# Decode attention and MLP on one core: the next head's softmax weights move behind the copy of the output column, and the scores use 4 stationary columns instead of 32

## The chip, the core and the metric

The kernel runs on one core of a Trainium2 chip. Its engines are TensorE (PE, with its weight loads shown apart as PEld), VectorE (DVE), ScalarE (ACT), GpSimd (POOL) and SyncE (SP), whose queue issues nearly all transfers here. The metric is device time in microseconds (us), lower is better. A profile is one execution with a hardware trace.

## The reference

Two layers of attention and MLP run one after the other, and then both again with the same weights: four token vectors (batch B = 4) of width D = 640, 32 heads of 128, the last W = 1024 cached keys and values of each head, everything in fp32.

```python
x = x + A(layernorm(x)); x = x + M(layernorm(x)); x = x + A(layernorm(x)); x = x + M(layernorm(x))
# A: q = (x @ wq) per head;  scores = q . k_cache[:, :, -1024:] * 128**-0.5
#    p = softmax(scores);    o = p @ v_cache[:, :, -1024:];   return o @ wo
# M: return relu(x @ w1) @ w2          (w1: 640 x 1728, w2: 1728 x 640)
```

## The kernel before

The host packs all that one head needs into a record: 9,472 fp32 columns on 128 partitions (4.85 MB), in the order WQ (640 columns), K (4,096), V (4,096), WO (640). Five records fit into SBUF (`slot0` to `slot4`), beside a `ring` of 8,960 columns that holds MLP weights and parts of one record.

The program makes two rounds (r = 0, 1) of attention and MLP. Round 0 takes heads 0 to 31. Round 1 begins with heads 27 to 31, which still lie in the slots, and then loads heads 0 to 26 again. All loads stand in one list, `items`, in a fixed order, and go to SP's queue: `pump()` issues the next one only when nothing live lies in its destination. `done(key, lo, hi)`, called behind the matmuls that used a piece, frees it and calls `pump()`. So a transfer can't begin before PE has used up what lies there, and all behind it in the list wait too. At the end of a round (`ending`) the last three records are split: K of head a, K of b, V of a, K of c, V of b, V of c in two halves; then come w1 in five pieces and w2. In round 0 the first five pieces of w1 and a bit of w2 fit into the ring; the rest of w2 needs the columns that the first MLP matmuls free.

Each engine executes in the order in which the code is written (`InOrder`). Per head, with n the position in the round:

- `query(n+2)`: 5 matmuls (10 as profiled: each fp32 matmul shows as two instructions) into `misc`, then DVE copies `misc` to `qT`.
- `scores(n+1)`: 8 matmuls into `sc_ps[(n+1) % 2]`, one column group of 32 partitions for each batch entry b. The stationary operand is column b of `qT` repeated 32 times, so that all 32 partitions of the group hold the same scores. DVE takes the maximum, ACT the exponential with its sum in `tot`.
- `weights(n+1)`: DVE takes the reciprocal of the sum, makes `mrt` from it, and transposes the exponentials in two halves (into PSUM `t_ps`, then scaled into `wT`).
- `values(n)`: 8 matmuls of `wT` with V into `o_ps`; then four DVE operations gather the column `on` out of `o_ps`.
- `output_T(i)`: a matmul of `on` with `pick`, and DVE's copy of the result to `oTs`; `project`: 4 matmuls of `oTs` with WO into `acc`, which frees the slot.

Around the MLP stand `center` (the mean for the layer norm) and `mlp`. `busy(n)` is a matmul with one stationary column and n moving columns whose result nobody uses. In round 0 the last 3 heads are projected behind the loop (`late`), in round 1 the last one.

Of the kernel before, what the change touches and what calls it, by code (L numbers as in the profile page):

```python
# [38 lines left out]
P = 128  # L39
# [53 lines left out]
def decode_kernel(ctx: ExitStack, tc: tile.TileContext, xf, rec, w1, w2, out):  # L93
    nc = tc.nc
    pe, dve, act, pool, sp = (InOrder(tc, e) for e in (nc.tensor, nc.vector, nc.scalar, nc.gpsimd, nc.sync))
# [5 lines left out]
    scratch = sb.tile([P, 480], F32, name="scratch")  # L101
    wT = scratch[:, :128].rearrange("p (i c j) -> p i c j", i=2, c=16)
    on = scratch[:, 128:256]
    xc = scratch[:, 256:256 + FD]
    x_sb = scratch[:, :FD]
    hT = scratch.rearrange("p (m j) -> p m j", j=32)
    oTs = sb.tile([P, LATE, B], F32, name="oTs")
    qT = sb.tile([P, B], F32, name="qT")
# [5 lines left out]
    nmax, rtot, rstd, eps, eps_dh, ones, unused, sums, squares, tot0, tot1 = (small[:, i:i + 1] for i in range(11))  # L114
    tot = [tot0, tot1]
# [3 lines left out]
    sc_ps = [ps.tile([P, W], F32, name=f"sc_ps{i}") for i in range(2)]  # L119
# [25 lines left out]
    dve.memset(eps_dh, EPS * DH)  # L145
    dve.memset(ones, 1.0)
    dve.memset(o_ps, 0.0)

    order = [list(range(H)), list(range(H - NS, H)) + list(range(H - NS))]
    LAST = H - NS  # L150

    def home(h, r):

        return h % NS if not r or h >= LAST else (h - 6 + LAST) % NS
# [30 lines left out]
    n = 0  # L185
# [24 lines left out]
    n = 0  # L210
# [18 lines left out]
    def cols(key, lo, n):  # L229

        for x, y, buf, col in pieces(key):
            if x <= lo and lo + n <= y:
                return buffers[buf][:, col + lo - x:col + lo - x + n]
        raise KeyError((key, lo, n))

    def done(key, lo, hi):

        if key[0] == "rec" and key[1] == 0 and key[2] >= LAST:
            return
        for x, y, buf, col in pieces(key):  # L240
            a, b = col + max(lo, x) - x, col + min(hi, y) - x
            if a < b:
                rest = []
                for bb, u, v in live:
                    if bb != buf or v <= a or b <= u:
                        rest.append((bb, u, v))
                    else:
                        rest += [(bb, p, q) for p, q in ((u, a), (b, v)) if p < q]
                live[:] = rest
        pump()  # L250


    def busy(n):

        pe.matmul(sc_ps[1][0:1, :n], mean_of[:, 0:1], slot[home(LAST, 0)][:, K:K + n], start=True, stop=True)

    def center(fill):

        x = acc[:, :FD]
        dve.tensor_reduce(sums, x, op=OP.add, axis=AX.X)  # L260
        if fill:
            busy(256)
        pe.matmul(misc[:, 0:1], mean_of, sums, start=True, stop=True)
        if fill:
            busy(512)
            busy(256)
        dve.tensor_scalar(xc, x, misc[:, 0:1], None, op0=OP.subtract)
        dve.transpose(xT, xc)
        act.activation(t_ps[:, :FD], xc, AF.Square, accum_out=squares)
# [7 lines left out]
    def scale_scores():  # L277

        pe.matmul(o_ps[:, 8:8 + B], ones.to_broadcast([P, P]), mrt, start=True, stop=True)
        dve.tensor_tensor(mrt, o_ps[:, 8:8 + B], of_batch, op=OP.mult)  # L280
        dve.tensor_reduce(sums, mrt, op=OP.add, axis=AX.X)
        act.activation(rstd, sums, AF.Sqrt, bias=eps_dh, scale=float(DH))
        act.activation(unused, eps, AF.Exp)
# [4 lines left out]
    def query(r, h):  # L288
        key = ("rec", r, h)
        for k in range(KB):  # L290
            pe.matmul(misc[:, 8:8 + B], cols(key, WQ + k * DH, DH), xblock(k), start=(k == 0), stop=(k == KB - 1))
        done(key, WQ, K)
        dve.tensor_copy(qT, misc[:, 8:8 + B])

    def scores(r, h, s, first=False):
        key = ("rec", r, h)
        for i in range(2):
            for b in range(B):
                pe.matmul(sc_ps[s][32 * b:32 * b + 32, 512 * i:512 * i + 512], qT[:, b:b + 1].to_broadcast([P, 32]),
                          cols(key, K + 512 * (B * i + b), 512), start=True, stop=True)  # L300
            done(key, K + VH * i, K + VH * i + VH)
        dve.tensor_reduce(nmax, sc_ps[s], op=OP.max, axis=AX.X, negate=True)
        if first:
            dve.reciprocal(rstd, rstd)
        dve.tensor_tensor(nmax, nmax, rstd, op=OP.mult)
        act.activation(sc_ps[s], sc_ps[s], AF.Exp, bias=nmax, scale=rstd, accum_out=tot[s])

    def weights(s):
        dve.reciprocal(rtot, tot[s])
        dve.tensor_scalar(mrt, of_batch, rtot, None, op0=OP.mult)  # L310
        for i in range(2):
            dve.transpose(t_ps, sc_ps[s][:, 512 * i:512 * i + 512])
            dve.tensor_tensor(wT[:, i], t_ps.rearrange("p (c j) -> p c j", j=32)[:, :, :B],
                              mrt.unsqueeze(1).to_broadcast([P, 16, B]), op=OP.mult)

    def values(r, h):
        key = ("rec", r, h)
        for i in range(2):
            for g in range(4):
                pe.matmul(o_ps[32 * g:32 * g + 16, :], wT[:, i, 4 * g:4 * g + 4, :].rearrange("p c j -> p (c j)"),  # L320
                          cols(key, V + VH * i + 512 * g, 512), start=(i == 0), stop=(i == 1))
            done(key, V + VH * i, V + VH * i + VH)
        dve.tensor_scalar(on, o_ps[:, :DH], of_block[:, 0:1], None, op0=OP.mult)
        for c in range(1, 4):
            dve.scalar_tensor_tensor(on, o_ps[:, DH * c:DH * c + DH], of_block[:, c:c + 1], on, op0=OP.mult, op1=OP.add)

    def output_T(i):
        pe.matmul(o_ps[:, :B], on, pick, start=True, stop=True)
        dve.tensor_copy(oTs[:, i], o_ps[:, :B])

    def project(r, h, i, end):
        key = ("rec", r, h)
        for n in range(NB):
            pe.matmul(acc[32 * n:32 * n + B, :FD], oTs[:, i], cols(key, WO + n * FD, FD),
                      start=False, stop=end, skip_group_check=True)
        done(key, WO, REC)
# [39 lines left out]
    for r in range(2):  # L376
        hs = order[r]
        late = LATE if r == 0 else 1
        center(r > 0)
        dve.tensor_scalar(mrt, mean_of[:, :B], squares, None, op0=OP.mult)  # L380
        query(r, hs[0])
        scale_scores()
        scores(r, hs[0], 0, True)
        query(r, hs[1])
        weights(0)
        for n, h in enumerate(hs):
            more = n + 1 < H
            i = n - (H - late)
            if more:
                scores(r, hs[n + 1], (n + 1) % 2)  # L390
            values(r, h)
            if more:
                weights((n + 1) % 2)
            if n + 2 < H:
                query(r, hs[n + 2])
            if i < 0:
                output_T(0)
                project(r, h, 0, False)
            elif more:
                output_T(i)  # L400
        for i in range(late):
            if i == max(0, late - 2):
                output_T(late - 1)
            project(r, hs[H - late + i], i, i == late - 1)
        center(True)
        mlp(r)
# [40 lines left out]
```

## Time and profile before

| | |
|---|---|
| median of 3 runs | 757.75 us (755.97 to 761.33) |
| the profiled execution | 753.13 us, span 751.4 us |
| PE busy | 538.2 us (72%) |
| DVE busy | 338.9 us (45%) |
| DMA, mean over the span | 304.48 MB, 405 GB/s |
| mean granted PE clock | 0.768 |

In the page's lines of slices each of 40 columns is 1/40 of the span (18.8 us); a digit is a share in tenths. In the table of windows the last three columns are the granted PE clock (1.00 is full speed), the busy share of the DMA engines and the bytes moved per time. In the timeline the columns are the start, the length, the engine, the instructions with their count, and in brackets the idle time of the engine just before with what ended it. Groups give the count, the busy time, the mean of one instruction in ns, and the idle time before them.

### The profile page before, as it was taken

The numbers are of one execution on the slowest core, as the hardware profiler recorded it, in microseconds if no ns is written. First come the engines' busy times: TensorE is split into PE (matmuls) and PEld (weight loads), VectorE is DVE, ScalarE is ACT, GpSimd is POOL, SyncE is SP. The second block draws the span as 40 slices with busy tenths as digits, with TensorE's granted clock in tenths as the row PEclk, the third lists the DMA queues.
The fourth block names the chain that finished last, engine by engine and source line by source line (L and its number), as shares of the span: only waits on it lengthen the run. The fifth ranks groups of instructions, "written<-read, shape, count | busy, mean of one in ns | idle before, by whom it ended". The sixth has DMA issues, their size and how long they took to land.

```text
span 751.4 us, 8825 instructions
## 1 busy us (share of the span) xinstructions
PE 538.2 (72%) x3704; PEld 222.6 (30%) x3704; DVE 338.9 (45%) x934; ACT 96.0 (13%) x154; POOL 1.1 (0%) x9
## 2 busy tenths in 40 slices
PE   3375686876676776777699777777776777776868
PEld 2132243233233232233224233323322233232312
DVE  2435535445535445345512655555555435345450
ACT  2101101101101101101111111111111101101111
POOL 0000000000000000000000000000000000000000
PEclk9768757677877678668679988868778757777689
DMA  9999999999999999999939997999999999999991
GB/s 388 426 441 420 442 428 420 446 423 428 437 424 437 431 422 443 424 424 423 387 125 407 366 432 319 414 428 422 440 427 432 432 424 437 431 426 424 423 420 64
DMA packets 15335, 304.48 MB, mean 405 GB/s; under 512 B 1712, under 2 KB 1984, under 8 KB 5312
## 3 DMA queue, kind: packets, MB, share of 16 engines
q1 hardware_dynamic: 15264, 303.91, 95.2%
q8 instruction: 29, 0.48, 0.3%
q14 instruction: 10, 0.08, 0.0%
q10 hardware_dynamic: 32, 0.01, 0.0%
HBM read 303.84 MB, written 0.08 MB: 404 GB/s over the span
## 4 chain that ended last, share of the span: by engine, by line
DMA 55%; PE 29%; DVE 13%; issue 1%; ACT 0%; another core or an unknown queue 0%
DMA slot<-rec 55%; PE sc_ps L85 13%; PE o_ps L85 8%; DVE scratch L85 6%; DVE t_ps L85 4%; PE acc L85 4%; PE misc L85 4%; DVE mrt L85 1%; DVE small L85 1%; DVE oTs L85 1%; ACT sc_ps L85 0%; DVE qT L85 0%; DVE sc_ps L85 0%
## 5 line engine op out<-in xcount | busy, mean ns | idle before, releaser
L85 PE MATMUL sc_ps<-slot,qT 128*32 128x512 f32 x992 | 200.6, 951 | 2.9 <-DVE oTs L85 2.0
L85 PE MATMUL misc<-xT,slot 128*128 128x4 f32 x620 | 98.7, 286 | 123.4 <-DMA slot<-rec 122.5
L85 DVE TENSOR_REDUCE small<-sc_ps 128x1 f32<-128x1024 f32 x64 | 78.4, 1224 | 233.6 <-PE sc_ps L85 233.6
L85 ACT ACTIVATE sc_ps<-sc_ps,small 128x1024 f32<-128x1024 f32 (+3 forms) x70 | 77.5, 1107 | 593.1 <-DVE small L85 571.0
L85 PE MATMUL o_ps<-slot,scratch 128*16 128x512 f32 x1010 | 149.8, 715 | 2.7 <-DVE oTs L85 1.9
L85 PEld LDWEIGHTS misc<-xT,slot 128*128 128x128 f32 x620 | 93.3, 233 | 178.5 <-DMA slot<-rec 160.0
L85 DVE STREAM_TRANSPOSE t_ps<-sc_ps 128x512 f32<-128x512 f32 x128 | 93.2, 728 | 2.2
L85 PE MATMUL acc<-slot,oTs 128*4 128x160 f32 x512 | 39.3, 393 | 54.5 <-DVE oTs L85 54.5
L85 PEld LDWEIGHTS o_ps<-slot,scratch 128*16 128x16 f32 x1010 | 37.4, 126 | 137.8 <-issue 131.8
L85 DVE SCALAR_TENSOR_TENSOR scratch<-o_ps,of_block,scratch 128x128 f32<-128x128 f32 x192 | 67.3, 351 | 6.8
L85 PEld LDWEIGHTS sc_ps<-slot,qT 128*32 128x32 f32 x992 | 43.6, 155 | 80.1 <-issue 71.9
L85 DVE TENSOR_SCALAR scratch<-o_ps,of_block 128x128 f32<-128x128 f32 x64 | 22.4, 350 | 50.6 <-PE o_ps L85 50.6
L85 PE MATMUL o_ps<-pick,scratch 128*128 128x4 f32 x128 | 29.1, 298 | 15.5 <-DVE scratch L85 15.5
L85 DVE COPY qT<-misc 128x4 f32<-128x4 f32 x64 | 10.1, 157 | 50.8 <-PE misc L85 50.5
L85 PEld LDWEIGHTS o_ps<-pick,scratch 128*128 128x128 f32 x128 | 25.5, 247 | 21.7 <-DVE scratch L85 21.7
L85 DVE TENSOR_TENSOR scratch<-t_ps,mrt 128x64 f32<-128x64 f32 x128 | 28.8, 225 | 4.4
L85 PE MATMUL sc_ps<-slot,mean_of 128*1 128x512 f32 (+1 forms) x54 | 26.2, 590 | 0.0
L85 PEld LDWEIGHTS acc<-slot,oTs 128*4 128x4 f32 x512 | 7.4, 85 | 61.5 <-DVE oTs L85 60.0
L85 DVE TENSOR_SCALAR mrt<-of_batch,small 128x4 f32<-128x4 f32 x64 | 14.7, 230 | 2.3
L85 DVE RECIPROCAL small<-small 128x1 f32<-128x1 f32 x68 | 10.4, 153 | 8.8 <-ACT small L85 7.5
L85 DVE COPY oTs<-o_ps 128x4 f32<-128x4 f32 x64 | 10.1, 158 | 7.7 <-PE o_ps L85 6.7
L85 ACT ACTIVATION_READ_ACCUMULATOR sc_ps<-sc_ps,small 128x1 f32 x64 | 12.2, 191 | 0.0
(53 smaller groups left out, 97.2 us busy)
## 6 DMA issues: line engine op xcount, KB each, us to landing
slot<-rec SPq DMA_DIRECT2D x46, 4736.0 KB, 30.7
slot<-rec SPq DMA_DIRECT2D x17, 2368.0 KB, 14.3
slot<-rec SPq DMA_DIRECT2D x5, 1024.0 KB, 33.1
ring<-w SPq DMA_DIRECT2D x5, 864.0 KB, 13.6
slot<-rec SPq DMA_DIRECT2D x2, 2048.0 KB, 40.3
slot<-rec SPq DMA_DIRECT2D x3, 1344.0 KB
slot<-w SPq DMA_DIRECT2D x3, 864.0 KB, 31.7
ring<-rec SPq DMA_DIRECT2D x1, 2368.0 KB
```

The costliest lines, as they stand in the source:

```text
L85: r = build(*args, **kwargs)
```

## The change

Three things change. In the loop over heads, `weights(n+1)` moves from before `query(n+2)` to the end of the iteration, behind `output_T` and `project`. The stationary operand of the scores has 4 columns instead of 32, so that only partitions 32b to 32b+3 get scores; the others are set to zero once at the start, and the sum of partition 32b is spread over its block by a 32x32 transpose of `tot` (read as 32 equal columns) into `spread`. And two `busy(512)` stand ahead of the last `output_T` of each round.

```diff
+    spread = scratch[:, 256:288]
...
+    for a in sc_ps:
+        dve.memset(a, 0.0)
...
-                pe.matmul(sc_ps[s][32 * b:32 * b + 32, 512 * i:512 * i + 512], qT[:, b:b + 1].to_broadcast([P, 32]),
+                pe.matmul(sc_ps[s][32 * b:32 * b + 4, 512 * i:512 * i + 512], qT[:, b:b + 1].to_broadcast([P, 4]),
...
     def weights(s):
-        dve.reciprocal(rtot, tot[s])
+
+        dve.transpose(spread, tot[s].to_broadcast([P, 32]))
+        dve.reciprocal(rtot, spread[:, 0:1])
         dve.tensor_scalar(mrt, of_batch, rtot, None, op0=OP.mult)
...
             values(r, h)
-            if more:
-                weights((n + 1) % 2)
             if n + 2 < H:
                 query(r, hs[n + 2])
             if i < 0:
                 output_T(0)
                 project(r, h, 0, False)
             elif more:
                 output_T(i)
+            if more:
+                weights((n + 1) % 2)
         for i in range(late):
             if i == max(0, late - 2):
+                busy(512)
+                busy(512)
                 output_T(late - 1)
             project(r, hs[H - late + i], i, i == late - 1)
```

On DVE, one head in the middle of round 0 stands like this before. The first rows are the four operations that gather the output column `on` (in `scratch`), the next six are `weights`, the last two the copies to `qT` and `oTs`.

```order
L85 TENSOR_SCALAR scratch<-o_ps,of_block 128x128
L85 SCALAR_TENSOR_TENSOR scratch<-o_ps,of_block,scratch 128x128 x3
L85 RECIPROCAL small<-small 128x1
L85 TENSOR_SCALAR mrt<-of_batch,small 128x4
L85 STREAM_TRANSPOSE t_ps<-sc_ps_78 128x512
L85 TENSOR_TENSOR scratch<-t_ps,mrt 128x64
L85 STREAM_TRANSPOSE t_ps<-sc_ps_78 128x512
L85 TENSOR_TENSOR scratch<-t_ps,mrt 128x64
L85 COPY qT<-misc 128x4
L85 COPY oTs<-o_ps 128x4
```

The same place on DVE after the change:

```order
L85 TENSOR_SCALAR scratch<-o_ps,of_block 128x128
L85 SCALAR_TENSOR_TENSOR scratch<-o_ps,of_block,scratch 128x128 x3
L85 COPY qT<-misc 128x4
L85 COPY oTs<-o_ps 128x4
L85 STREAM_TRANSPOSE scratch<-small 128x32
L85 RECIPROCAL small<-scratch 128x1
L85 TENSOR_SCALAR mrt<-of_batch,small 128x4
L85 STREAM_TRANSPOSE t_ps<-sc_ps_78 128x512
L85 TENSOR_TENSOR scratch<-t_ps,mrt 128x64
L85 STREAM_TRANSPOSE t_ps<-sc_ps_78 128x512
L85 TENSOR_TENSOR scratch<-t_ps,mrt 128x64
```

Both copies now stand directly behind the gathering, the weights stand behind the copies, and the small transpose of the sum is new.

On PE the order is unchanged but for the end of each round. At the end of round 0 it was, from the values of the last head on:

```order
L85 MATMUL o_ps<-slot_72,scratch 16x512 x8
L85 MATMUL acc<-slot_75,oTs 4x160 x4
L85 MATMUL o_ps<-pick,scratch 128x4
L85 MATMUL acc<-slot_71,oTs 4x160 x4
L85 MATMUL acc<-slot_72,oTs 4x160 x4
```

And after the change:

```order
L85 MATMUL o_ps<-slot_72,scratch 16x512 x8
L85 MATMUL acc<-slot_75,oTs 4x160 x4
L85 MATMUL sc_ps_78<-slot_73,mean_of 1x512 x2
L85 MATMUL o_ps<-pick,scratch 128x4
L85 MATMUL acc<-slot_71,oTs 4x160 x4
L85 MATMUL acc<-slot_72,oTs 4x160 x4
```

The two `busy` matmuls stand between the projection of the third last head and `output_T` of the last one. SP's and ACT's orders are the same in both.

## Prediction

> **What bounds the kernel now.** I read the page's slices, queues and chain first: which stage is bound by what.
>
> ```profile
> DMA  9999999999999999999939997999999999999991
> GB/s 388 426 441 420 442 428 420 446 423 428 437 424 437 431 422 443 424 424 423 387 125 407 366 432 319 414 428 422 440 427 432 432 424 437 431 426 424 423 420 64
> ...
> q1 hardware_dynamic: 15264, 303.91, 95.2%
> ...
> DMA 55%; PE 29%; DVE 13%; issue 1%; ACT 0%; another core or an unknown queue 0%
> ```
>
> Transfers run at 420 to 445 GB/s nearly everywhere: 303.91 MB at 426 are 713 us, 38 less than the span. So nothing can be won while the DMA is full, and all that can be won lies where it isn't: the dip in the middle (125, then 366 and 319), and the end (64). The windows price these places; the last column is GB/s, the third last the granted PE clock.
>
> ```profile
> 290.00:300.00 10.00, 7.30 (x56) 2.61 (x51) 5.14 (x14) 1.29 (x2) 0.00 (x0) 0.79 1.00 426
> 370.00:380.00 10.00, 5.34 (x36) 1.66 (x36) 4.99 (x15) 0.47 (x2) 0.00 (x0) 0.64 0.50 203
> 380.00:390.00 10.00, 10.00 (x61) 2.72 (x62) 1.38 (x5) 1.97 (x4) 0.00 (x0) 0.68 0.23 76
> 420.00:430.00 10.00, 7.57 (x64) 3.07 (x60) 5.03 (x14) 1.29 (x2) 0.00 (x0) 0.83 0.90 359
> 430.00:440.00 10.00, 7.57 (x64) 3.11 (x60) 5.04 (x14) 1.29 (x2) 0.00 (x0) 0.88 0.95 379
> 460.00:470.00 10.00, 7.51 (x68) 3.04 (x64) 5.88 (x15) 1.29 (x2) 0.00 (x0) 0.93 0.64 248
> 740.00:750.00 10.00, 7.82 (x125) 3.44 (x121) 1.16 (x4) 1.08 (x3) 0.00 (x0) 1.00 0.03 9
> ```
>
> A window at g GB/s loses 10 x (1 - g/426) us: 5.2 and 8.2 us between 370 and 390, 1.6, 1.1 and 4.2 us between 420 and 470. At the end PE works on without transfers. In all three places the DMA waits for PE to free space, or has nothing left. How long PE takes for a head there, the timeline shows (start, length, engine; in brackets the idle time before):
>
> ```profile
> 341.14 1.12 DVE L85 SCALAR_TENSOR_TENSOR scratch<-o_ps,of_block,scratch 128x128 f32<-128x128 f32 x3
> 342.18 0.15 DVE L85 RECIPROCAL small<-small 128x1 f32<-128x1 f32 x1
> 342.32 0.39 PE L85 MATMUL o_ps<-pick,scratch 128*128 128x4 f32 x2 [0.43 <-DVE scratch L85]
> 344.29 0.23 DVE L85 TENSOR_TENSOR scratch<-t_ps,mrt 128x64 f32<-128x64 f32 x1
> 344.50 0.15 DVE L85 COPY oTs<-o_ps 128x4 f32<-128x4 f32 x1
> 344.71 0.46 PE L85 MATMUL acc<-slot,oTs 128*4 128x160 f32 x8 [2.00 <-DVE oTs L85]
> 344.98 3.23 PE L85 MATMUL sc_ps<-slot,qT 128*32 128x512 f32 x16
> 363.94 2.79 PE L85 MATMUL sc_ps<-slot,qT 128*32 128x512 f32 x12 [2.02 <-DVE oTs L85]
> ```
>
> `output_T` on PE is over at 342.71, but DVE copies its result only at 344.50: `weights`, from the reciprocal at 342.18 on, stands ahead of the copy. PE stands for 2.00 us. From 344.71 to 363.94 two heads pass, 9.6 us each. Where DMA is the bound, the same wait is small, since `weights` is over before the next record lands:
>
> ```profile
> 275.60 1.28 PE L85 MATMUL misc<-xT,slot 128*128 128x4 f32 x10 [2.92 <-DMA slot<-rec]
> 277.35 0.71 PE L85 MATMUL acc<-slot,oTs 128*4 128x160 f32 x8 [0.26 <-DVE oTs L85]
> ```
>
> **The change, part by part.** *The move.* Behind it the projection should wait 0.26 us as in the last row, not 2.00: 1.74 us less per head that PE bounds. `weights` now runs while PE does the next `scores`. It takes 344.52 - 342.18 = 2.34 us, the first half of `wT` some 1.0 us earlier; the scores take 3.23 us here and 1.72 at full clock (below), with 0.46 of projection ahead. So `values` find their first half ready, just so at full clock. Where DMA bounds, PE waits 2.92 us per record and the weights fit under the scores: nothing. Queued behind the waiting copy on DVE is `weights` alone, and its reader, `values`, stands behind the scores on PE anyway.
>
> The second effect is the clock. Groups of three heads at the end of each round, and the same work at full clock out of the chain:
>
> ```profile
> L85 PE MATMUL sc_ps<-slot,qT 128*32 128x512 f32 x48 | 9.5, 930 | 2.0 <-DVE oTs L85 2.0
> L85 PE MATMUL o_ps<-slot,scratch 128*16 128x512 f32 x48 | 8.2, 811 | 0.0
> L85 PE MATMUL acc<-slot,oTs 128*4 128x160 f32 x16 | 0.9, 299 | 4.0 <-DVE oTs L85 4.0
> ...
> L85 PE MATMUL sc_ps<-slot,qT 128*32 128x512 f32 x48 | 9.2, 904 | 0.0
> L85 PE MATMUL o_ps<-slot,scratch 128*16 128x512 f32 x48 | 6.8, 696 | 0.0
> L85 PE MATMUL acc<-slot,oTs 128*4 128x160 f32 x24 | 1.9, 401 | 6.0 <-DVE oTs L85 6.0
> ```
>
> ```profile
> 716.49 1.72 PE sc_ps L85 x16
> 718.21 1.76 PE o_ps L85 x16
> ```
>
> At full clock three heads would take 3 x (1.72 + 1.76) = 10.4 us; they take 17.7 us at 344.7 to 370.3 and 16.0 at 695.1 to 720: 7.3 and 5.6 us go to the half clock. It follows the gap:
>
> ```profile
> 342.00:344.00 2.00, 0.39 (x2) 0.30 (x2) 1.90 (x6) 0.00 (x0) 0.00 (x0) 1.00 0.97 411
> 346.00:348.00 2.00, 2.00 (x16) 0.45 (x12) 0.00 (x0) 0.00 (x0) 0.00 (x0) 0.50 1.00 425
> 387.00:404.00 17.00, 16.33 (x169) 5.32 (x161) 1.32 (x5) 1.25 (x4) 0.00 (x0) 1.00 0.95 358
> ```
>
> PE idles at 342 to 344, and 2 us later the clock is 0.50. Without the gap I expect it to stay near 1.00. The Trainium skill, in "TensorE: Matmul & The Clock Gate", section "Why this matters for your kernels", has the clock fall only behind idle gaps of over about 3 us. By that rule gaps of 2.0 us would cost no clock and closing them would give none; the rows disagree. I keep it as a rival.
>
> *The first end (round 0).* Three waits (2.0 + 4.0 us in the group) give 3 x 1.74 = 5.2, the clock up to 7.3: 12.5. But the last V must land first.
>
> ```profile
> 332.10 2.30 PE misc L85 x10
> ...
> 374.17 3.61 PE L85 MATMUL o_ps<-slot,scratch 128*16 128x512 f32 x16 [1.94 <-DVE oTs L85]
> 379.41 0.59 PE L85 MATMUL o_ps<-pick,scratch 128*128 128x4 f32 x2 [1.10 <-DVE scratch L85]
> 386.64 0.33 SPq L85 DMA_DIRECT2D ring<-w  x1
> ...
> 682.34 1.42 PE L85 MATMUL misc<-xT,slot 128*128 128x4 f32 x10 [4.11 <-DMA slot<-rec]
> 724.15 3.51 PE L85 MATMUL o_ps<-slot,scratch 128*16 128x512 f32 x16
> ```
>
> At 332.10 the last whole record has landed. Behind it come three K parts (4,736 columns with WQ) and three V parts (4,096): 26,496 columns of 512 bytes, 13.57 MB, 31.9 us at 426 GB/s, so the last V lands at about 364 (an estimate). The last `values` start at 374.17, ten later than that. Their start behind `output_T`'s copy gains nothing (weights now follow the copy; the first half of `wT` is ready about when the copy was), so three waits it is, and I take 10.5 of the 12.5, between 5.2 (no clock) and 12. The first w2 transfer, issued at 386.64 when the MLP frees the ring, moves up as much. The queue, empty from about 376 on, then hardly runs dry.
>
> *Round 1.* In five heads from 416 to 457 the projection waits 10.1 us:
>
> ```profile
> L85 PE MATMUL acc<-slot,oTs 128*4 128x160 f32 x40 | 2.6, 335 | 10.1 <-DVE oTs L85 10.1
> ```
>
> 5 x 1.74 = 8.7 us, without any clock. The three dips there are 6.9 us in sum, and what ends each is a slot or the ring coming free behind these heads. I take 6.5, from 4 to 7. Then the DMA is full until the end.
>
> *The second end (round 1).* The same three waits, 5.2, and up to 5.6 of clock: 10.8. The landing bound: from 682.34, three K and three V parts, all with WO: 28,416 columns, 14.55 MB, 34.2 us, to 716.5; the last `values` start at 724.15, 7.6 later, and then run at half clock (3.51). I take 9, from 5 to 10, some of it being the end's clock. The DMA ends earlier than PE here, so the whole comes off the end.
>
> *The rest.* The new 128x32 transpose isn't in the trace; the nearest is
>
> ```profile
> L85 DVE STREAM_TRANSPOSE xT<-scratch 128x160 f32<-128x160 f32 x4 | 1.4, 345 | 0.1
> ```
>
> so at most 0.35 us, at least 0; I take 0.2, being a fifth of the columns with a fixed part. It lies under the scores; where it doesn't (the last weights of a round, two times) it costs 0.4 in all; uncovered in all of some 14 heads that PE bounds (4, 6 and 4 at the three places) it would cost up to 2.8 us more. The two memsets run while x is on its way at the start. The scores' 4 columns stream the same 512 moving columns: I take 0, a gain on the weight loads (off the path) or loss being possible only through the clock (rival three). The two `busy` fill the gap of 1.10 us ahead of 379.41: at half clock they take about 1.7 (0.6 late), and they may bring the clock up before the MLP; net 0, from -1.5 to +1.2 in both rounds.
>
> Sum: 10.5 + 6.5 + 9 - 0.4 = 25.6; with 1 us that the clock gives in the MLP behind the busy matmuls, 26.6 us. The profiled execution, 753.13 (span 751.4 and 1.7 around it), becomes 726.5. The median, 757.75, lies 4.6 above that execution, which I carry over: 731.
>
> **The rivals.** *The clock does not follow the gap* (the page's rule above; or it falls on the remaining gaps of 0.4 + 0.3 us and the query's small matmuls). Then the waits alone count: 5.2 + 6.5 + 5.2 = 17 us, 741. For it: windows of 0.50 also where PE shows full, as at 346; against it: each follows a gap by one or two us.
>
> *The transfers hide it.* 55% of the chain is DMA; if the ends wait for landings rather than PE, nothing moves, 755 to 758. Against it: 10 and 7.6 us between last landing and last `values`, and a DMA that stands still from 376 to 387.
>
> *Slower: the 4-column scores don't count as activity.* If what sets the clock counts columns of the array in use, the scores with an eighth of the columns look idle and PE stays at half clock. A head is then 0.7 (projection) + 3.4 (scores) + 3.6 (values, 374.17) + 2.3 (query, 332.10) + 0.6 + 0.3 = 10.9 us against 9.6, so 1.3 in each of those 14 heads: 18 slower, 776. It decides once the clock in these heads is under about 0.65. Against it: from 387 to 404 PE runs only matmuls with 4 columns and one column, at 1.00.
>
> **How the numbers follow.** Forecast 0.60 (24 to 31 us gained: 727 to 734), clock rival 0.24 (735 to 745), no change 0.09, slower 0.05, still faster 0.02. A measurement here tells about 1% (7.6 us) from no change. Faster by over 1%: 0.86; within: 0.08; slower: 0.06. The range takes in the forecast and the clock rival, with the runs' own spread of 3 us: 723 to 746.
>
> **What would show it.** Right: the projection's idle in a head falls from 2.0 to about 0.3 us; clock near 1.00 at the former 344 to 370; no window under 350 GB/s between 376 and 470 but for a short dip at the MLP; last `values` within 3 us of the last landing. Wrong: clock rows of 0.50 through the scores, `values` waiting for `wT`, or a head in the DMA-bound part over the 11.4 us that its 4.85 MB take at 426 GB/s.

## The result and the profile after

The changed kernel takes 727.6 us in the median (726.1 to 729.35), the kernel before beside it 756.86 us: ratio 0.961, 95% interval 0.956 to 0.966, so 29.3 us faster by the medians. The prediction said 731 us, with 723 to 746 as its range. The profiled execution took 727.87 us (span 726.2) against 753.13 (751.4): 25.2 us less in the span, 26.6 were forecast.

The same lines of the page as before, now of the kernel after: DMA share in 40 slices, what it moved, its queue, and the chain of waits.

```profile
DMA  9999999999999999999999999999999999999994
GB/s 385 430 425 429 432 433 433 435 431 431 432 431 432 429 431 428 427 427 426 419 361 405 394 423 429 436 430 433 431 432 431 433 430 427 434 429 420 423 422 205
...
q1 hardware_dynamic: 15264, 303.91, 98.3%
...
DMA 74%; PE 20%; DVE 4%; issue 1%; ACT 0%; SPq 0%
```

The dip to 125 GB/s in the middle is now 361, the ones to 319 and 366 are gone or shallow, and the last slice holds 205 instead of 64. The share of DMA in the chain rose from 55% to 74%. The windows of the places where time was lost:

```profile
350.00:360.00 10.00, 8.78 (x68) 2.86 (x61) 7.38 (x21) 1.30 (x2) 0.00 (x0) 0.84 1.00 420
370.00:380.00 10.00, 9.97 (x75) 3.03 (x74) 1.39 (x5) 1.97 (x4) 0.00 (x0) 0.99 0.87 324
410.00:420.00 10.00, 9.32 (x68) 3.13 (x60) 6.59 (x17) 1.29 (x2) 0.00 (x0) 0.77 0.97 368
420.00:430.00 10.00, 8.65 (x88) 4.52 (x88) 8.24 (x26) 2.59 (x4) 0.00 (x0) 1.00 1.00 425
460.00:470.00 10.00, 6.00 (x60) 2.49 (x52) 7.01 (x21) 2.59 (x4) 0.00 (x0) 0.96 1.01 434
```

370 to 380 loses 2.4 us by the prediction's formula and 410 to 420 1.4; before, the first pair of windows lost 13.4 and round 1 another 6.9. One head near the end of round 0, in the timeline:

```profile
342.75 0.38 PE L85 MATMUL o_ps<-pick,scratch 128*128 128x4 f32 x2 [0.43 <-DVE scratch L85]
343.17 0.16 DVE L85 COPY oTs<-o_ps 128x4 f32<-128x4 f32 x1 [0.41 <-PE o_ps L85]
343.25 0.20 DVE L85 STREAM_TRANSPOSE scratch<-small 128x32 f32<-128x32 f32 x1
343.39 0.46 PE L85 MATMUL acc<-slot,oTs 128*4 128x160 f32 x8 [0.25 <-DVE oTs L85]
343.66 1.90 PE L85 MATMUL sc_ps<-slot,qT 128*4 128x512 f32 x16
345.38 1.90 PE L85 MATMUL o_ps<-slot,scratch 128*16 128x512 f32 x16
345.61 0.23 DVE L85 TENSOR_TENSOR scratch<-t_ps,mrt 128x64 f32<-128x64 f32 x1
345.75 1.22 DVE L85 TENSOR_REDUCE small<-sc_ps 128x1 f32<-128x1024 f32 x1
349.55 0.53 PE L85 MATMUL acc<-slot,oTs 128*4 128x160 f32 x8 [0.25 <-DVE oTs L85]
```

The projection waits 0.25 us instead of 2.00. Scores and values run at full clock, 1.72 us from start to start, and the head takes 6.16 us (343.39 to 349.55) instead of 9.6. `values` begin at 345.38 with no idle time ahead: the weights are covered. Not every head is like this one: the scores of the next head, from 349.83 on, take 3.59 us, and the clock of the window from 350 is 0.84. DVE has little idle time left either (345.61 to 345.75 and on, and 8.24 of 10 us busy in the window from 420); this comes back below.

### The profile page after: what moved, and what is told of

The parts are those of the page before. It is cut to its first block, busy times and chain, and to the rows that moved or that the text cites. A ratio compares the mean times of both kernels' runs of the same rounds, so it can differ in the third digit from the quotient of the medians.

```text
span 726.2 us, 8920 instructions
## 1 busy us (share of the span) xinstructions
PE 526.8 (73%) x3712; PEld 213.4 (29%) x3712; DVE 357.2 (49%) x1000; ACT 96.0 (13%) x154; POOL 1.1 (0%) x9
## 4 chain that ended last, share of the span: by engine, by line
DMA 74%; PE 20%; DVE 4%; issue 1%; ACT 0%; SPq 0%
DMA slot<-rec 74%; PE sc_ps L85 8%; PE o_ps L85 5%; PE misc L85 4%; PE acc L85 4%; DVE scratch L85 2%; DVE oTs L85 1%; ACT sc_ps L85 0%; DVE small L85 0%; DVE t_ps L85 0%; SPq L85 0%; DVE mrt L85 0%; SPq L82 0%; DVE sc_ps L85 0%; DVE qT L85 0%
## 5 line engine op out<-in xcount | busy, mean ns | idle before, releaser
L85 PE MATMUL misc<-xT,slot 128*128 128x4 f32 x620 | 102.8, 293 | 154.9 <-DMA slot<-rec 154.0
L85 PE MATMUL sc_ps<-slot,qT 128*4 128x512 f32 x992 | 196.7, 934 | 0.8 <-DVE qT L85 0.7
L85 PEld LDWEIGHTS misc<-xT,slot 128*128 128x128 f32 x620 | 97.4, 242 | 210.7 <-DMA slot<-rec 199.1
L85 PE MATMUL o_ps<-slot,scratch 128*16 128x512 f32 x1010 | 140.1, 673 | 4.3 <-DVE scratch L85 3.5
L85 PEld LDWEIGHTS o_ps<-slot,scratch 128*16 128x16 f32 x1010 | 34.1, 117 | 132.2 <-issue 81.2
L85 PEld LDWEIGHTS sc_ps<-slot,qT 128*4 128x4 f32 x992 | 33.8, 116 | 84.8 <-issue 74.3
L85 PE MATMUL acc<-slot,oTs 128*4 128x160 f32 x512 | 39.1, 390 | 15.5 <-DVE oTs L85 15.5
L85 PE MATMUL sc_ps<-slot,mean_of 128*1 128x512 f32 (+1 forms) x62 | 28.9, 571 | 0.0
L85 DVE STREAM_TRANSPOSE scratch<-small 128x32 f32<-128x32 f32 x64 | 12.9, 201 | 1.4 <-ACT sc_ps L85 1.4
```

Source lines behind the costliest of these rows:

```text
L85: r = build(*args, **kwargs)
```

## The experiments

Ratios are to the kernel before, timed beside each batch of runs. The first four runs (up to "The clock without the move") and the next four are two batches on the same chip; the kernel before took 756.5 us in the first and 752.3 us in the second. The last four were timed beside each other on another chip, where it took 754.5 us.

### The move alone

```diff
             values(r, h)
-            if more:
-                weights((n + 1) % 2)
             if n + 2 < H:
                 query(r, hs[n + 2])
...
+            if more:
+                weights((n + 1) % 2)
```

> Only the move of the weights; scores with 32 stationary columns, no transpose of the sum, no added busy matmuls. My theory (the projection no longer waits 2.0 us, the clock follows, the DMA's idle time goes): ratio to before 0.962 to 0.969, the projection's idle time before a head's project 0.25 us. If the narrow stationary operand did the work instead: ratio 0.98 to 1.00. If the waits alone count and the clock does not follow: 17 us, ratio 0.977.

Measured: 726.5 us, ratio 0.961 (0.956 to 0.966). The move alone gives all that the change gives, a little more than I had expected; the 0.977 of the waits alone lies outside the interval. Its projection waits 15.5 us in 61 heads as in the changed kernel, 0.25 each.

### The 4 columns and the transpose alone

```diff
+    spread = scratch[:, 256:288]
...
+    for a in sc_ps:
+        dve.memset(a, 0.0)
...
-                pe.matmul(sc_ps[s][32 * b:32 * b + 32, ...], qT[:, b:b + 1].to_broadcast([P, 32]),
+                pe.matmul(sc_ps[s][32 * b:32 * b + 4, ...], qT[:, b:b + 1].to_broadcast([P, 4]),
...
-        dve.reciprocal(rtot, tot[s])
+        dve.transpose(spread, tot[s].to_broadcast([P, 32]))
+        dve.reciprocal(rtot, spread[:, 0:1])
```

> Only the 4 stationary columns with the transpose of the sum, the weights stay ahead of the copy of the output column. My theory: the scores take as long as with 32 columns at the same clock (1.72 us at full clock), and the transpose of 0.20 us lies ahead of the copy, so each of some 14 heads that PE bounds loses 0.2 us: ratio 1.000 to 1.005. If narrow operands paid: ratio 0.985 or less. If they counted less for the clock: mean clock under 0.75 and ratio over 1.01.

Measured: 762.25 us, ratio 1.009 (1.006 to 1.013): slower, and more so than expected. The groups of the projection, first of the kernel before, then of this one:

```profile
L85 PE MATMUL acc<-slot,oTs 128*4 128x160 f32 x512 | 39.3, 393 | 54.5 <-DVE oTs L85 54.5
```

```profile
L85 PE MATMUL acc<-slot,oTs 128*4 128x160 f32 x512 | 40.0, 400 | 69.4 <-DVE oTs L85 69.4
L85 DVE STREAM_TRANSPOSE scratch<-small 128x32 f32<-128x32 f32 x64 | 12.9, 201 | 1.4 <-ACT sc_ps L85 1.4
```

The transpose takes 0.20 us as I took it, and in a head that PE bounds the wait is 2.25 instead of 2.00. The price is more than my sum allows: where the DMA isn't full I had counted 14 heads, and 14 x 0.25 is 3.5 us, 0.5%, below the interval. Two differences of the traces can hold the rest, and no run here separates them. After a wait of 2.00 us the scores of the next head ran wholly at full clock (1.90 us) in 5 of 20 heads of the kernel before, and after 2.25 us in none of 24 (2.74 to 3.64 us). And in round 1 the DMA stands longer: by the prediction's formula the windows from 420 to 490 lose 14 us in the profiled execution of this run (763.1 us) and 8 in that of the kernel before (753.1 us). The largest dip, of the kernel before and then of this run:

```profile
460.00:470.00 10.00, 7.51 (x68) 3.04 (x64) 5.88 (x15) 1.29 (x2) 0.00 (x0) 0.93 0.64 248
```

```profile
460.00:470.00 10.00, 7.93 (x52) 2.84 (x52) 4.62 (x13) 1.29 (x2) 0.00 (x0) 0.67 0.36 125
```

The mean clock of the profiled execution is 0.76 against 0.768, and that of all timed executions 0.760 to 0.775 against 0.754 to 0.783. So the narrow operand shows no loss of clock; the run with all fillers and 4 columns and the one with 32, below, compare the two with nothing else changed but the transpose.

### Without the two busy matmuls

```diff
             if i == max(0, late - 2):
-                busy(512)
-                busy(512)
                 output_T(late - 1)
```

> The changed kernel without the two busy matmuls ahead of the last output column. My theory (they bring the clock up before the MLP): 1 to 3 us slower than the changed kernel, ratio to before 0.962 to 0.966, the clock 0.50 in center and the first block of the MLP. If they only fill idle time: the same as the changed kernel within 0.5 us, 0.960 to 0.961.

Measured: 727.37 us, ratio 0.962 (0.957 to 0.967). The window with `center` and the MLP's first block, of this run, of the changed kernel, and of the move alone, which has no busy matmuls there either:

```profile
370.00:380.00 10.00, 10.00 (x62) 3.06 (x63) 1.39 (x5) 1.97 (x4) 0.00 (x0) 0.68 0.71 264
```

```profile
370.00:380.00 10.00, 9.97 (x75) 3.03 (x74) 1.39 (x5) 1.97 (x4) 0.00 (x0) 0.99 0.87 324
```

```profile
370.00:380.00 10.00, 9.96 (x76) 3.00 (x76) 1.47 (x6) 1.97 (x4) 0.00 (x0) 1.00 0.93 351
```

Without them the clock is 0.68 there instead of 0.99, and the DMA moves 264 GB/s instead of 324, as my theory says. But the move alone has 1.00 and 351 GB/s without them. So the full clock there doesn't need them, and that they raise it rests on one pair of executions. In the time the kernels can't be told apart.

### The clock without the move

`bound(r, n)` holds for n >= 26, and in round 1 for n <= 12 too; `filler` is a matmul of one stationary column, here with 512 moving ones.

```diff
                 output_T(0)
+                for _ in range(3 if bound(r, n) else 0):
+                    filler(r, h, n, 512)
                 project(r, h, 0, False)
```

> The kernel before, with three matmuls of one stationary and 512 moving columns, whose result nobody uses, in the 2.0 us gap ahead of the projection, in the heads near the ends of the rounds. The wait itself stays. If the clock follows the gap: clock near 1.00 in these heads, scores and values of three heads 10.4 us instead of 17.7 and 16.0, in all 8 to 14 us faster, ratio 0.982 to 0.990. If the clock does not follow the gap: not faster, up to 6 us slower where the fillers run at half clock, ratio 1.000 to 1.008.

Measured: 744.29 us, ratio 0.984 (0.978 to 0.989), 12 us faster although the wait stays and PE has more to do. The last row is from right behind these two heads, where nothing is projected and so no fillers stand:

```profile
340.00:350.00 10.00, 9.55 (x75) 4.23 (x67) 6.34 (x16) 1.30 (x2) 0.00 (x0) 1.00 1.01 427
350.00:360.00 10.00, 9.46 (x72) 4.91 (x68) 6.22 (x19) 2.59 (x4) 0.00 (x0) 1.00 0.99 415
...
L85 PE MATMUL sc_ps<-slot,qT 128*32 128x512 f32 x32 | 4.3, 597 | 0.0
L85 PE MATMUL o_ps<-slot,scratch 128*16 128x512 f32 x32 | 4.2, 592 | 0.0
...
362.76 3.64 PE L85 MATMUL sc_ps<-slot,qT 128*32 128x512 f32 x16 [2.03 <-DVE oTs L85]
```

The clock is 1.00 in both windows, and the scores of two heads take 597 ns in the mean; in the group of the kernel before, it was 930. Behind the gap of 2.03 us that is left there, the scores take 3.64 us, at half clock. So the gap was what halved the clock. That settles the first rival. By the rule of the Trainium skill ("TensorE: Matmul & The Clock Gate", "Why this matters for your kernels"), which warns of gaps over about 3 us, gaps of 2.0 us would be too short to cost clock; here they did, and filling them gave 12 us.

### What the cover of the weights is worth

```diff
     def weights(s):
-        dve.transpose(spread, tot[s].to_broadcast([P, 32]))
+        for _ in range(6):
+            dve.transpose(spread, tot[s].to_broadcast([P, 32]))
```

> The changed kernel with the transpose of the sum done six times instead of once, 1.0 us more on VectorE per head, ahead of the weights. My theory (the weights are covered by the projection and the scores, with some 0.4 to 0.5 us of slack at full clock): 1.0 us uncovered two times in the last weights of a round, about 0.5 us in a head at full clock, 2 to 5 us slower than the changed kernel, ratio to before 0.963 to 0.968. If nothing covers the weights: 1.0 us in each of 14 to 20 heads, ratio 0.979 or more.

Measured: 732.91 us, ratio 0.975 (0.972 to 0.978), 1.3 to 1.5% more than the changed kernel (0.962, below, and 0.961), so 9 to 11 us. This lies above my 2 to 5 us and below the 0.979 of no cover at all; I had taken the cover for larger than it is. A head of this run:

```profile
411.28 1.44 DVE L85 STREAM_TRANSPOSE scratch<-small 128x32 f32<-128x32 f32 x6
411.42 0.46 PE L85 MATMUL acc<-slot,oTs 128*4 128x160 f32 x8 [0.26 <-DVE oTs L85]
...
414.12 2.08 PE L85 MATMUL o_ps<-slot,scratch 128*16 128x512 f32 x16 [0.54 <-DVE scratch L85]
414.87 0.22 DVE L85 TENSOR_TENSOR scratch<-t_ps,mrt 128x64 f32<-128x64 f32 x1
415.01 1.21 DVE L85 TENSOR_REDUCE small<-sc_ps 128x1 f32<-128x1024 f32 x1
...
418.53 0.46 PE L85 MATMUL acc<-slot,oTs 128*4 128x160 f32 x8 [0.26 <-DVE oTs L85]
```

DVE does 1.24 us more per head, and the head grows from 6.16 to 7.11 us (411.42 to 418.53). `values` wait 0.54 us for `wT`, as forecast; but the maximum for the next head also begins only when the weights are done (414.87 to 415.01), and everything behind it on DVE moves on. Of the 1.24 us only 0.29 found room, not the 0.4 to 0.5 that I had expected: at full clock DVE bounds the head almost as much as PE.

### The gaps that are left

Four more `busy(512)` around the last weights of a round (two ahead of `output_T`, two behind it, in the second last head; the second argument of `busy` names the `sc_ps` buffer that it writes):

```diff
+            for _ in range(2 if n == H - 2 else 0):
+                busy(512, 0)
             if i < 0:
                 output_T(0)
...
+            for _ in range(2 if n == H - 2 else 0):
+                busy(512, 0)
             if more:
                 weights((n + 1) % 2)
```

> The changed kernel with four more busy matmuls of 512 columns in the second last head of each round: two ahead of its output column, two behind it, where PE waits 1.6 us for the gathering and then for the last weights. If the half clock of the last values (3.61 us) and of the busy matmuls behind them comes from these gaps: the last values at 1.9 us, 2 to 4 us faster than the changed kernel, ratio to before 0.955 to 0.958. If the clock at the end has another cause: the same as the changed kernel, 0.960 to 0.962.

Measured: 723.15 us, ratio 0.961 (0.958 to 0.964). As a ratio that is no gain over the changed kernel's 0.961, where I had expected 0.955 to 0.958. But the last values are shorter, as these rows of the changed kernel and then of this run show (the last query, the values of the second last head, and the last ones):

```profile
687.02 1.69 PE L85 MATMUL misc<-xT,slot 128*128 128x4 f32 x10 [1.89 <-DMA slot<-rec]
693.29 2.52 PE L85 MATMUL o_ps<-slot,scratch 128*16 128x512 f32 x16
699.56 3.61 PE L85 MATMUL o_ps<-slot,scratch 128*16 128x512 f32 x16 [0.76 <-DVE scratch L85]
```

```profile
685.22 1.28 PE L85 MATMUL misc<-xT,slot 128*128 128x4 f32 x10 [1.37 <-DMA slot<-rec]
690.98 1.91 PE L85 MATMUL o_ps<-slot,scratch 128*16 128x512 f32 x16 [1.84 <-DMA slot<-rec]
697.07 1.95 PE L85 MATMUL o_ps<-slot,scratch 128*16 128x512 f32 x13
```

But the values of the second last head now wait 1.84 us for their V: a part of what PE saves goes into the wait for the landing. With one filler of 256 columns more in each head near the ends, in the 0.43 us ahead of `output_T`:

```diff
+                if bound(r, n) and n < H - 2:
+                    filler(r, h, n, 256)
                 output_T(0)
```

> As the run before, and one matmul of 256 moving columns more in each head near the ends of the rounds, in the 0.4 us in which PE waits for the gathering ahead of the output column. If these small gaps still cost clock: clock 1.00 in these heads, scores of the last head 1.9 instead of 3.6 us, 1 to 3 us faster than the run with the last gap alone, ratio to before 0.951 to 0.956. If the landing of the last V sets the end by then: no faster than that run.

Measured: 723.05 us, ratio 0.961 (0.958 to 0.964), the same. In this window the clock is 1.00 where it was 0.77:

```profile
410.00:420.00 10.00, 9.49 (x92) 3.88 (x95) 8.41 (x27) 1.58 (x4) 0.00 (x0) 1.00 1.00 425
```

Not everywhere: from 350 to 360 it is 0.84 as in the changed kernel, and from 690 to 700 it is 0.77. No time is gained, where I had expected 0.951 to 0.956 if these gaps counted. The DMA is full in the window above (425 GB/s), which fits my second case, that the landings set the end. The move alone with all these fillers and the two busy matmuls:

> The move alone, with 32 stationary columns, and all the fillers of the run with all gaps filled. If 4 columns matter neither for PE nor for the clock: the same as that run within 2 us, better by the 0.2 us of the transpose two times; ratio to before 0.950 to 0.956. If 32 columns keep the clock up better: clearly faster than it.

Measured: 723.69 us, ratio 0.961 (0.959 to 0.964): not to be told from the two runs ahead of it. From the run before it this one differs only in the columns and the transpose, so the number of columns matters neither way.

### Side by side on one chip

As the kernel before was faster in the second batch too, four kernels were timed again beside each other.

> The changed kernel unaltered, so that the next runs can be compared with it on one chip. If the ratio depends on the chip's transfer rate: between 0.955 and 0.966.

> The move alone again, beside the changed kernel on one chip. My theory (the move is all that counts; the transpose of 0.2 us lies on a VectorE that is nearly full at full clock, the two busy matmuls give back about as much): within 2 us of the changed kernel. If the other two edits pay together: 3 us slower or more; if they cost: 3 us faster or more.

> The changed kernel with the last gaps filled, beside the changed kernel on one chip. From the last K's landing to the end its trace took 36.0 us (685.2 to 721.2) against 39.2 (687.0 to 726.2) of the changed kernel: if that holds, 2 to 4 us faster than it. If the transfers fix the end: the same within 1 us.

> The move alone with all fillers, beside the changed kernel on one chip. If the clock at the ends is what is left: 3 to 5 us faster than the changed kernel. If the landing of the last records sets the ends now: no faster than the run with only the last gaps filled.

| kernel | median us | ratio | 95% interval |
|---|---|---|---|
| changed | 725.51 | 0.962 | 0.958 to 0.966 |
| move alone | 727.87 | 0.964 | 0.960 to 0.968 |
| changed, last gaps filled | 723.24 | 0.959 | 0.955 to 0.963 |
| move alone, all fillers | 724.32 | 0.960 | 0.956 to 0.964 |

All these intervals overlap, but each holds the spread of the kernel before as well. Directly compared, the six runs with the last gaps filled (723.07 to 724.82 us) are, but for one, faster than every run of the changed kernel (724.28 to 727.07): 2.3 us by the medians, as expected if its shorter end holds. The move alone is 2.4 us slower than the changed kernel by the medians, a little over the 2 us that I had allowed, but its runs (723.80 to 729.18) lie on both sides. With all fillers it is some 3.5 us faster than without, 1.2 us faster than the changed kernel where I had expected 3 to 5, and no faster than the last gaps filled. That fits the second case again: with the last gaps filled the landings leave nothing more to win here.

## Why the prediction was right

By its steps, from the places of the same event in the two profiles:

**The bound.** "Nothing can be won while the DMA is full" held: the slices of the DMA-bound part of round 1 read 414 to 440 GB/s before and 420 to 436 after. In round 0 the query that stood at 332.10, where the last whole record has landed, still does:

```profile
332.33 1.96 PE L85 MATMUL misc<-xT,slot 128*128 128x4 f32 x10 [1.79 <-DMA slot<-rec]
...
365.42 2.57 PE L85 MATMUL o_ps<-slot,scratch 128*16 128x512 f32 x16 [1.72 <-DVE scratch L85]
```

So all the heads ahead of it gave nothing.

**The first end.** Forecast 10.5 us, and 1 us more from the busy matmuls' clock. The first w2 transfer that waits for the ring is issued when the MLP frees it:

```profile
375.19 9.67 SPq L85 DMA_DIRECT2D ring<-w  x6
```

at 386.64 before, so 11.45 us earlier. The sum is right, its two parts are not, and that they cancel is luck. The last `values` moved from 374.17 to 365.42 (the row above), 8.75 us, where 10.5 were forecast. The stretch from there to the transfer fell from 12.47 to 9.77 us, 2.7 where 1 was forecast. Nor is it shown that the busy matmuls give the second part, since the move alone has the full clock there without them. By the prediction's own working from 332.33 the last V lands at about 364.2 (an estimate), 1.2 us ahead of the last `values`: so near the landing hardly more of the 12.5 could be had.

**Round 1.** Forecast 6.5. The query of the first of the last four heads, released by the landing of its record, started at 682.34 before and now at

```profile
664.20 2.29 PE L85 MATMUL misc<-xT,slot 128*128 128x4 f32 x10 [2.45 <-DMA slot<-rec]
```

18.14 us earlier, of which 11.45 came from the first end: 6.7 us, as forecast.

**The second end.** Forecast 9, and part of the 1 us above. From that query to the end of the span it takes 62.0 us instead of 69.1: 7.1 us. This term was too large. The waits went: up to the last `values` it takes 35.4 us instead of 41.8, and by the prediction's working the last V lands at 664.20 + 34.2 = 698.4 (an estimate), 1.2 us ahead of them. But the end's clock, of which I had taken a part on top, gave only 0.6 us behind that point. PE waits 1.89 us for the last K at 687.02 (its row stands above), and then runs scores and values at half clock for the most part.

```profile
689.88 3.64 PE L85 MATMUL sc_ps<-slot,qT 128*4 128x512 f32 x16
693.29 2.52 PE L85 MATMUL o_ps<-slot,scratch 128*16 128x512 f32 x16
699.56 3.61 PE L85 MATMUL o_ps<-slot,scratch 128*16 128x512 f32 x16 [0.76 <-DVE scratch L85]
```

A gap that PE closes elsewhere opens again at the landing; I had counted the landing as a bound in time only. Whether it costs clock differs from execution to execution. In another profiled one of the same kernel, on the other chip (725.51 us), PE waits 0.66 us for the last K, and the scores behind it run at full clock:

```profile
688.86 1.90 PE L85 MATMUL sc_ps<-slot,qT 128*4 128x512 f32 x16
```

Reckoned alike, that execution gives 11.7, 7.3 and 8.7 us for the three places, against 11.45, 6.7 and 7.1. So the miss of the third term is partly the execution.

**The small terms.** The transpose takes 0.20 us as taken, its place under the scores is shown by `values` without idle time, and the 4 columns are free. Three steps failed without changing the sum. The heads with a wait of about 2.0 us before were 4, 16 and 4 at the three places, not 4, 6 and 4. The gain didn't grow with the count: after the change a query waits for its record's landing from 471.77 on, before only from 569.18 on, so in the further heads the closed waits became waits for landings. The cover of the weights was thinner than "just so": DVE itself is nearly full at full clock. And the 1 us of clock from the busy matmuls isn't shown for certain by any run.

**The rivals.** That the clock doesn't follow the gap fell with the fillers in the gap (12 us from the clock alone). That the transfers hide the change fell with the result. That 4 columns don't count for the clock fell with the run of these alone, whose mean clock hardly moved, and with the all-filler runs, 723.05 us with 4 columns and 723.69 with 32. (The evidence against it in the prediction, 387 to 404, holds three instructions with 128 columns too, 0.7 us in all.)

**The signs.** The projection's wait fell to 0.25 us; the last `values` come 1.2 us behind the estimated landings; no window from 376 to 470 is under 350 GB/s but the dip at the MLP (324); records still land some 11.2 us apart. The clock at the former 344 to 370 is 0.84, not near 1.00, in two windows of three: this sign came true in part only.

**The median.** The medians differ by 29.3 us, the profiled executions by 25.3. The carried offset of 4.6 us between profile and median was there before, but not after (727.87 against 727.6), which is why the forecast median was 3.4 us too high although the forecast gain of the profiled execution was 1.3 us too large. That the two misses partly cancel in the median is luck too.

## What to carry to other kernels

In a kernel bound by transfers, look for the places where the transfer queue runs dry, and cost a change only there: the sum of those windows is the most that it can give. A wait of PE had two prices here, its own time and the half clock of the work behind it; a filler in the gap told the two apart. And compare parts, not only sums: the same event in both traces shows where two misses cancel. When work moves under another engine's cover, count the mover's whole round, not only when its first result is needed.

## What the runs showed of the hardware

In the kernel before, a PE gap of 2.0 us in a head of 9.6 us was followed by scores that ran in part or wholly at half clock in 15 of 20 heads (2.60 to 3.64 us for 16 instructions), and at full clock (1.90 us) in 5. Three matmuls of one stationary and 512 moving columns in the gap, whose result nobody used, kept the clock at 1.00 from 340 to 360. With gaps of 0.43 and 0.25 us per head it is mostly 1.00 and still falls now and then (0.84 from 350 to 360, 0.77 from 410 to 420); with 256 more moving columns in the first of them it was 1.00 in the last of these windows and 0.84 in the other. Scores with 4 stationary columns take as long as with 32 (1.90 us for 16 instructions at full clock), and with all fillers the two take the same time.
